# Code rows kept twice, and the mask products of a turn spread over eight 32x64 places: an attention and feed-forward kernel on one core

## The chip, the cores and the metric

The kernel runs on one core of a Trainium2 chip. The metric is the device time of one execution in microseconds (us). The engines are named as the profile names them: PE is TensorE (PEld its weight loads), DVE is VectorE, ACT is ScalarE, POOL is GpSimd, SP is SyncE, which here issues the transfers.

## What is computed

Attention in clusters, and then a feed-forward block. Every query and every key is assigned to the nearest of 16 centroids of its head; a query attends only to keys with the same assignment.

```python
batch, n_heads, seq, head_dim = (4, 8, 768, 64)      # q, k, v; n_clusters = 16
q_assign = np.argmax(np.einsum('bhsd,hcd->bhsc', q_n, c_n), axis=-1)
k_assign = np.argmax(np.einsum('bhsd,hcd->bhsc', k_n, c_n), axis=-1)
mask = q_assign[:, :, :, None] == k_assign[:, :, None, :]
scores = scale * np.matmul(q, k.transpose(0, 1, 3, 2))
scores = np.where(mask, scores, -1000000000.0)
attn = np.exp(scores - np.max(scores, axis=-1, keepdims=True))
attn = attn / (np.sum(attn, axis=-1, keepdims=True) + 1e-09)
out = np.matmul(attn, v)
# then, with x the heads side by side, (3072, 512)
h = x @ w_in                                         # (512, 2048)
return (h * (1.0 / (1.0 + np.exp(-1.702 * h)))) @ w_out
```

## The kernel before

The program has a fast path and a general one; the fast one runs, and the general one only if a check at the end says so. The fast path has two stages: attention (up to 353 us in the profile), and then the feed-forward block (L743 and L800), which the change doesn't touch.

**Tiling of the attention.** Heads are handled in pairs: 4 batches x 4 pairs = 16 pairs, the two heads of a pair (a = 0, 1) lying in partitions 0 to 63 and 64 to 127. For a pair, `T[p, 0]` and `T[p, 1]` hold queries and keys with the head dimension on the partitions. The queries of a pair are taken in two halves of 384, the keys in six blocks of 128; one half with one key block is a *unit*, 12 units a pair, 192 in all. Scores stand with keys on the partitions and queries along the row, for both heads: a PSUM tile `s` of 128 x 2 x 384, of which two exist, each head in a bank of its own.

**A turn** is two units. There are 96 turns, and the order of the work in them is written out by hand (L658 to L696):
- L453, `scores`: for each unit four fp32 products of 64 rows and 64 columns with 384 queries, one for each head and each half of the key block. An fp32 product leaves two records in the profile, so a turn has 16.
- L476, `part`: into the same PSUM tile the mask is added, again four products for each unit, in bf16, eight a turn (L467 in the first pair, see below).
- L484, `exps`: ScalarE takes the exponential of the unit, 128 x 768, to a tile `A`, of which there are four.
- L502, `add_up`: GpSimd adds up the exponentials over the key blocks (one of the twelve units goes to VectorE at L495).
- L518, `values`: exponentials of the turn before times the values, eight fp32 products of 64 rows and 64 columns, 16 records.
- Once in three turns L535 makes the row sums (128 rows, 64 columns) and VectorE normalises (L545 to L557), L527 copies the result out of PSUM; once in six L329 makes the products with the centroids for the next pair (128 rows, 32 columns), from which VectorE makes the assignments (L352 to L389). Between these, ScalarE and VectorE check and round the weights of the feed-forward block, step by step (L189 to L230).

**The mask.** Each key and query has a code, rank x 2^50 with ranks 1 to 16 for the clusters. For codes x (query) and y (key) the product is to be xy - x²/2 - y²/2 = -(x - y)²/2: nothing where they are equal, and hugely negative elsewhere. From the second pair on this is a product with three rows that count: on the key side y, y²'s multiple and the constant -0.5 x 2^50, on the query side x, the constant and x²'s multiple. They stand in tiles `rows_of[w, i]` (w = 0 for queries, 1 for keys; i changes with the pair), in the 64 partitions of their head, at 0, 1 and 32, and the other partitions are zero: the product at L476 takes all 64. The constants and zeros are written once at the start by GpSimd (L297, L299). The codes come for each pair through DRAM (`line`): four transfers at L398 write them, eight at L404 read them, one row of 768 each, issued by SyncE during the pair before.

The first pair's mask is made otherwise: L467 multiplies rows of 16 (one for each cluster) with 128 columns, four products a turn.

Names used for the prediction's steps: the *last turn's* `A` must be finished before L518; `s` of a unit must be read by L484 before the L453 two units later writes it again; `A` comes free when L518 and L502 have read it.

Of the kernel before, what the change touches and what calls it, by code (L numbers as in the profile page):

```python
# [18 lines left out]
def kernel(  # L19
    tc: tile.TileContext,  # L20
    q: bass.AP,
    k: bass.AP,
    v: bass.AP,
    centroids: bass.AP,
    moe_w_in: bass.AP,
    moe_w_out: bass.AP,
    out: bass.AP,
):

    args = (q, k, v, centroids, moe_w_in, moe_w_out, out)
    bad = fast(tc, *args)
    with tc.If(bad > 0):
        general(tc, *args)
# [3 lines left out]
def fast(  # L39
# [26 lines left out]
    nc = tc.nc  # L66

    B, H, S, D = q.shape
    NC = centroids.shape[1]
    DM, DF = moe_w_in.shape  # L70
    P = 128
# [10 lines left out]
    CODE = float(2 ** 50)  # L82
    NX = 6 * HP
    SQ = 32
# [137 lines left out]
    def check_w(i, raw, z):  # L222
# [39 lines left out]
    rows_of = {(w, i): hp1.tile([P, S], BF16, name=f"rows{w}{i}")  # L262
               for w in range(2) for i in range(2)}
# [22 lines left out]
    for a in range(2):  # L286
        rows = slice(a * D, (a + 1) * D)
        nc.vector.tensor_copy(
            out=cT[rows, :, a, :],
# [5 lines left out]

    for (w, _), rows in rows_of.items():
        nc.gpsimd.memset(rows, 0.0)  # L297
        for r in range(SQ * w, P, D):
            nc.gpsimd.memset(rows[r:r + 1, :], -0.5 * CODE)  # L299

    T, code, sT, hots = {}, {}, {}, {}

# [90 lines left out]
    def prep_spread(p):  # L393
        n = NJ * 4
        row = code.pop(p)
        line = dram.tile([2, n, P], BF16, name="line")
        for r in range(0, P, SQ):
            nc.sync.dma_start(  # L398
                out=line[:, :, r:r + SQ].rearrange("b n t -> n b t"),
                in_=row[r:r + n])  # L400
        for a in range(2):
            for w, b, to in ((0, 0, 1), (0, 1, SQ), (1, 0, 1), (1, 1, 0)):
                at, r = (w * 2 + a) * NJ, a * D + to
                nc.sync.dma_start(  # L404
                    out=rows_of[w, p % 2][r:r + 1, :],
                    in_=line[b, at:at + NJ, :].rearrange(
                        "j t -> (j t)")[None, :])

    def prep_hot(p):

# [18 lines left out]
    def hot_w(w, h, n):  # L429
# [3 lines left out]
    PREP = [lambda p, i=i: prep_turn(p, i) for i in range(4)]  # L433
    PREP += [prep_near, prep_assign,
             lambda p: (prep_hot if p == 0 else prep_spread)(p)]


# [5 lines left out]
    def split(g):  # L443
        return divmod(g, 2)
# [15 lines left out]
    def part(u):  # L460

        g, kt = divmod(u, NJ)
        p, h = split(g)
        if p == 0:
            for a in range(2):
                r = SQ * a
                nc.tensor.matmul(  # L467
                    out=s_of[u][:, a, :],
                    lhsT=hots[1][r:r + NC, kt * P:(kt + 1) * P],
                    rhs=hots[0][r:r + NC, h * HALF:(h + 1) * HALF],  # L470
                    start=False, stop=True)
            return
        for a in range(2):
            rows = slice(a * D, (a + 1) * D)
            for c in range(0, P, D):
                nc.tensor.matmul(  # L476
                    out=s_of[u][c:c + D, a, :],
                    lhsT=rows_of[1, p % 2][rows, kt * P + c:kt * P + c + D],
                    rhs=rows_of[0, p % 2][rows, h * HALF:(h + 1) * HALF],
                    start=False, stop=True)  # L480
# [156 lines left out]
    for p in range(1, NPAIR):  # L637
        for i in range(2 if p == 1 else 0, len(PREP)):
            t = 2 * TG * (p - 1) + (0, 0, 0, 0, 1, 2, 2)[i]
# [18 lines left out]
    for t in range(NT + 2):  # L658
# [5 lines left out]
        for u in us:  # L664
            part(u)
# [638 lines left out]
```

## Time and profile before

| | us |
|---|---|
| median of 3 runs | 939.36 (939.26 to 939.95) |
| profiled execution | 939.74 |
| its span | 937.8 |
| attention stage in it | to 353 |

A profile shows one execution. Busy time of an engine is the time in which any of its instructions runs. Matmuls are pipelined: their records overlap, and their ends are modelled, so the distance from the start of one group to the start of the next tells what a group costs. "64*64" is rows x columns of the stationary operand. A wait is put down to what ended it last.

Busy in one pair of the middle (205.2 to 225.7 us, 20.5 us): PE 20.36, DVE 18.43, ACT 14.46, POOL 18.50. Of the groups of instructions, these matter beside the ones that the prediction shows:

| line | what | count | mean ns |
|---|---|---|---|
| L453 | scores, 64*64, 64x384 fp32 | 1536 records | 494 |
| L518 | values, 64*64, 64x384 fp32 | 1536 records | 483 |
| L535 | row sums, 128*64, 128x384 fp32 | 128 records | 511 |
| L329 | centroids, 128*32, 128x192 fp32 | 240 records | 332 |
| L484 | exponential, 128x768 | 192 | 804 |
| L502 | additions, 128x384 fp32 | 252 + 32 | 1091, 1061 |
| L299 | memset of one row of 768 | 8 | 734 |
| L297 | memset of 128 rows of 768 | 4 | 742 |

### The profile page before, as it was taken

How to read it: one execution, taken by the hardware profiler on the slowest of the kernel's cores; microseconds unless marked ns; L12 is line 12 of the kernel's file. 1: busy time of each engine (PE TensorE's matmuls, PEld its weight loads, DVE VectorE, ACT ScalarE, POOL GpSimd, SP SyncE). 2: the span in 40 equal slices, each digit the busy share in tenths (PEclk: the TensorE clock that was granted, in tenths of full speed). 3: DMA queues.
4: the chain of work that ended last, by engine and by line, in shares of the span. 5: the costliest groups of instructions: out<-in, count | busy, mean ns of one | idle time of the engine just before them, and what ended most of it. 6: DMA issues, size and time to landing. Idle time of an engine off the chain costs nothing.

```text
span 937.8 us, 16591 instructions
## 1 busy us (share of the span) xinstructions
PE 920.5 (98%) x6469; PEld 578.4 (62%) x6469; DVE 624.0 (67%) x1077; ACT 326.0 (35%) x703; POOL 420.8 (45%) x440
## 2 busy tenths in 40 slices
PE   6999999999999999999999999999999999999997
PEld 2344444444444445558886557887557887556886
DVE  3999999989988896775345775344776343677331
ACT  3667767767776672221001221001222000232000
POOL 5899899899999996772001220001211000120000
PEclk9999999999999999999999999999999999999999
DMA  9465556566543210011000000000000000000000
GB/s 184 101 128 101 99 103 138 106 121 114 103 99 98 81 49 10 0 29 40 23 23 22 1 0 1 23 23 24 0 1 1 23 23 23 0 1 1 23 24 26
DMA packets 138215, 46.65 MB, mean 50 GB/s; under 512 B 127256, under 2 KB 132496, under 8 KB 138128
## 3 DMA queue, kind: packets, MB, share of 16 engines
q1 hardware_dynamic: 137984, 45.48, 22.1%
q8 instruction: 53, 0.87, 0.4%
q14 instruction: 34, 0.28, 0.1%
q10 hardware_dynamic: 144, 0.03, 0.0%
HBM read 37.44 MB, written 8.05 MB: 49 GB/s over the span
## 4 chain that ended last, share of the span: by engine, by line
PE 84%; POOL 4%; DVE 4%; issue 3%; ACT 2%; DMA 1%; SPq 1%; ACTq 0%; DVEq 0%; POOLq 0%
PE b L800 31%; PE b L743 31%; PE s L453 9%; PE o L518 7%; POOL sum L502 4%; PE m L535 2%; PE s L476 2%; ACT A L484 1%; PE m L329 1%; DMA line<-row 0%; DVE x L556 0%; SPq L404 0%; DMA raw<-in_moe_w_out_dram 0%; DVE e L200 0%; PE m L315 0%
## 5 line engine op out<-in xcount | busy, mean ns | idle before, releaser
L502 POOL TENSOR_TENSOR sum<-sum,A 128x384 f32<-128x384 f32 x252 | 266.2, 1091 | 33.6 <-ACT A L484 21.3
L589 POOL TENSOR_TENSOR W<-w_in 128x256 f32<-128x256 f32 x32 | 23.3, 729 | 379.6 <-PE b L743 379.4
L484 ACT ACTIVATE A<-s 128x768 f32<-128x768 f32 x192 | 145.1, 804 | 99.4 <-PE s L476 76.3
L734 DVE TENSOR_TENSOR G<-b,G 128x384 f32<-128x384 f32 x224 | 124.4, 556 | 62.7 <-PE b L743 50.4
L453 PE MATMUL s<-T,T 64*64 64x384 f32 x1536 | 145.8, 494 | 2.7 <-ACT A L484 0.7
L734 DVE TENSOR_TENSOR y<-b,y 128x256 f32<-128x256 f32 x72 | 29.5, 423 | 171.7 <-PE b L800 121.8
L518 PE MATMUL o<-A,inv 64*64 64x384 f32 x1536 | 141.5, 483 | 0.0
L579 ACT ACTIVATE th<-G 128x384 f32<-128x384 f32 x128 | 67.0, 523 | 208.8 <-DVE G L734 128.5
L580 DVE SCALAR_TENSOR_TENSOR G<-th,G 128x384 f32<-128x384 f32 x128 | 91.3, 713 | 23.0 <-ACT th L579 19.1
L453 PEld LDWEIGHTS s<-T,T 64*64 64x64 f32 x1536 | 52.7, 132 | 79.0 <-ACT A L484 51.3
L743 PE MATMUL b<-x,W 128*128 128x384 f32 x256 | 93.0, 486 | 0.0
L743 PE MATMUL b<-T,w_in 128*128 128x384 f32 x256 | 93.0, 486 | 0.0
L743 PE MATMUL b<-x,w_in 128*128 128x384 f32 x256 | 88.5, 486 | 0.0
L800 PE MATMUL b<-Z,G 128*128 128x256 f32 x384 | 86.8, 379 | 0.0
L800 PE MATMUL b<-w_out,G 128*128 128x256 f32 x384 | 84.8, 379 | 0.0
L518 PEld LDWEIGHTS o<-A,inv 64*64 64x64 f32 x1536 | 58.9, 133 | 38.3 <-issue 33.2
L800 PEld LDWEIGHTS b<-w_out,G 128*128 128x128 f32 x384 | 72.8, 190 | 10.9
L800 PEld LDWEIGHTS b<-Z,G 128*128 128x128 f32 x384 | 73.0, 190 | 9.9
L743 PEld LDWEIGHTS b<-x,W 128*128 128x128 f32 x256 | 48.6, 190 | 33.9
L743 PEld LDWEIGHTS b<-T,w_in 128*128 128x128 f32 x256 | 48.6, 190 | 33.9
L743 PEld LDWEIGHTS b<-x,w_in 128*128 128x128 f32 x256 | 48.6, 190 | 33.6 <-issue 0.6
L810 ACT COPY y<-b 128x256 f32<-128x256 f32 x12 | 4.5, 372 | 141.5 <-PE b L800 141.5
(120 smaller groups left out, 1130.6 us busy)
## 6 DMA issues: line engine op xcount, KB each, us to landing
raw<-in_moe_w_in_dram SPq DMA_DIRECT2D x16, 512.0 KB
raw<-in_moe_w_out_dram SPq DMA_DIRECT2D x16, 512.0 KB
inv<-in_v_dram SPq DMA_DIRECT2D x16, 384.0 KB
in<-in_q_dram SPq DMA_DIRECT2D x60, 96.0 KB
in<-in_k_dram SPq DMA_DIRECT2D x60, 96.0 KB
out_dram<-y SPq DMA_DIRECT2D x12, 256.0 KB
out_dram<-y SPq DMA_DIRECT2D x24, 128.0 KB
rows<-line SPq DMA_DIRECT2D x120, 1.5 KB
```

The source lines that it names most:

```text
L453: nc.tensor.matmul(out=ps[c:c + D, a, 0:HALF], lhsT=T[p, 1][rows, kt * P + c:kt * P + c + D], rhs=T[p, 0][rows, h * HALF:(h + 1) * HALF], ...
L476: nc.tensor.matmul(out=s_of[u][c:c + D, a, :], lhsT=rows_of[1, p % 2][rows, kt * P + c:kt * P + c + D], rhs=rows_of[0, p % 2][rows, h * HA ...
L484: nc.scalar.activation(out=A_of[u], in_=s_of.pop(u), func=AF.Exp, scale=SCALE)
L502: nc.gpsimd.tensor_tensor(out=sum_of[g][:, a], in0=(A_of[u - 1] if kt == 1 else sum_of[g])[:, a], in1=A_of[u][:, a], op=ALU.add)
L518: nc.tensor.matmul(out=o_of[g][a * D:(a + 1) * D, r, 0:HALF], lhsT=v_in[p][rows, a, kt, :], rhs=A[rows, a, :], start=(kt == 0), stop=(kt = ...
L535: nc.tensor.matmul(out=ps[a * D:(a + 1) * D, 0:HALF], lhsT=twos, rhs=sm[:, a, :], start=(i == 0), stop=(i == len(parts) - 1))
L579: nc.scalar.activation(out=t, in_=h, func=AF.Tanh, scale=1.702)
L580: nc.vector.scalar_tensor_tensor(out=g, in0=t, scalar=1.0, in1=h, op0=ALU.add, op1=ALU.mult)
L589: engine.tensor_tensor(out=o, in0=a, in1=b, op=(ALU.add if op == "+" else ALU.subtract))
L734: nc.vector.tensor_tensor(out=o, in0=p, in1=a, op=ALU.add)
L743: nc.tensor.matmul(out=ps[:, 0:HALF], lhsT=a[:, c], rhs=x(c), start=(c == 0), stop=(c == 1))
L800: nc.tensor.matmul(out=ps[:, 0:DN], lhsT=a(f // 4)[:, f % 4], rhs=z(f), start=(f == 0), stop=(f == FB - 1))
```

## The change

The three rows of a head that count stand at 0, 1 and 2 in place of 0, 1 and 32, and they are kept twice: in partitions 0 to 2 and again in 32 to 34 of the head's 64. The product takes only these three rows, those of the first copy for the even unit of a turn and those of the second for the odd one. So the eight products of a turn have eight different places: four groups of rows (head and unit) by two groups of columns (half of the key block). Each transfer at L404 writes two partitions, 32 apart, from the same row of DRAM; the constants are written at four places of each of the four tiles in place of two, as one row (queries) or three (keys, of which two are overwritten by the codes). The first pair is as before.

```diff
     for (w, _), rows in rows_of.items():
         nc.gpsimd.memset(rows, 0.0)
-        for r in range(SQ * w, P, D):
-            nc.gpsimd.memset(rows[r:r + 1, :], -0.5 * CODE)
+        for r in range(0, P, SQ):
+            nc.gpsimd.memset(rows[r:r + 1 + 2 * w, :], -0.5 * CODE)
...
         for a in range(2):
-            for w, b, to in ((0, 0, 1), (0, 1, SQ), (1, 0, 1), (1, 1, 0)):
+            for w, b, to in ((0, 0, 1), (0, 1, 2), (1, 0, 1), (1, 1, 0)):
                 at, r = (w * 2 + a) * NJ, a * D + to
                 nc.sync.dma_start(
-                    out=rows_of[w, p % 2][r:r + 1, :],
+                    out=rows_of[w, p % 2][r:r + SQ + 1:SQ, :],
                     in_=line[b, at:at + NJ, :].rearrange(
-                        "j t -> (j t)")[None, :])
+                        "j t -> (j t)")[None, :].broadcast_to((2, S)))
...
         for a in range(2):
-            rows = slice(a * D, (a + 1) * D)
+            r = a * D + u % 2 * SQ
+            rows = slice(r, r + 3)
             for c in range(0, P, D):
                 nc.tensor.matmul(
                     out=s_of[u][c:c + D, a, :],
```

## The prediction, made before the changed kernel was run

> **What bounds the kernel now.** I read the page first, for the shares and for the chain that ended last.
>
> ```profile
> PE 920.5 (98%) x6469; PEld 578.4 (62%) x6469; DVE 624.0 (67%) x1077; ACT 326.0 (35%) x703; POOL 420.8 (45%) x440
> ...
> PE b L800 31%; PE b L743 31%; PE s L453 9%; PE o L518 7%; POOL sum L502 4%; PE m L535 2%; PE s L476 2%; ACT A L484 1%; PE m L329 1%; DMA line<-row 0%; DVE x L556 0%; SPq L404 0%; DMA raw<-in_moe_w_out_dram 0%; DVE e L200 0%; PE m L315 0%
> ```
>
> TensorE bounds it over the whole span, but the change lies in the attention stage alone, which ends at 353 us; from there L743 and L800 run as they do now. The mask products, L476, hold 2% of the chain. The groups by form give their durations, and beside them those of the first pair's mask products at L467, the only products in the trace with at most 32 rows:
>
> ```profile
> L476 PE MATMUL s<-rows,rows 64*64 64x384 bf16 x720 | 45.9, 323 | 0.9 <-DMA rows<-line 0.9
> ...
> L467 PE MATMUL s<-hots,hots 16*128 16x384 bf16 x24 | 3.2, 351 | 0.9 <-ACT hots L426 0.9
> ```
>
> 720 products in eights are 90 turns. What a turn costs is read in the timeline of TensorE, from start to start (first number start, second length to the modelled end of the last record):
>
> ```profile
> 203.52 1.47 PE L518 MATMUL o<-A,inv 64*64 64x384 f32 x16
> 205.13 1.57 PE L453 MATMUL s<-T,T 64*64 64x384 f32 x16
> 206.52 0.51 PE L476 MATMUL s<-rows,rows 64*64 64x384 bf16 x8
> ...
> 212.79 1.47 PE L453 MATMUL s<-T,T 64*64 64x384 f32 x16
> 214.08 0.51 PE L476 MATMUL s<-rows,rows 64*64 64x384 bf16 x8
> 214.40 1.47 PE L518 MATMUL o<-A,inv 64*64 64x384 f32 x16
> 215.69 1.47 PE L453 MATMUL s<-T,T 64*64 64x384 f32 x16
> ...
> 217.31 1.47 PE L518 MATMUL o<-A,inv 64*64 64x384 f32 x16
> 218.71 0.87 PE L535 MATMUL m<-sum,twos 128*64 128x384 f32 x4
> 219.50 1.52 PE L453 MATMUL s<-T,T 64*64 64x384 f32 x16
> ```
>
> A plain turn is 1.29 (L453) + 0.32 (L476) + 1.29 (L518) = 2.90 us. The eight mask products go in two rounds of four, 0.16 each; each lasts 0.32 and overlaps the next group, because all three lines use 64*64 operands. Where the operand's shape changes this overlap goes: L518 to L535 takes 217.31 to 218.71 = 1.40 instead of 1.29, though only the rows change (64 to 128, still 64 columns). L535 has two records in turn on each of its two places, 4 x 0.16 = 0.64, and takes 0.79 to the next line. So a change costs 0.11 to 0.15. The first pair's turns show a product of few rows between the same two neighbours:
>
> ```profile
> 26.36 1.47 PE L453 MATMUL s<-T,T 64*64 64x384 f32 x16
> 27.76 0.50 PE L467 MATMUL s<-hots,hots 16*128 16x384 bf16 x4
> 28.19 1.52 PE L518 MATMUL o<-A,inv 64*64 64x384 f32 x16
> 29.53 1.47 PE L453 MATMUL s<-T,T 64*64 64x384 f32 x16
> ```
>
> Here L453 takes 1.40, the mask 0.43 (two rounds of two, again 0.32 of streaming) and L518 1.34, because its first weights are no longer loaded ahead: 3.17 us, 0.27 more than a plain turn.
>
> **The change, part by part.** *Products in 32x64.* They take 3 rows where L453 and L518 keep 64, so I expect the change of shape twice in each of the 90 turns. The trace has no 32x64 product; the bounds come from the rows above.
> - L453 to L476: 1.40 instead of 1.29, +0.11.
> - L476 to L518: all eight in one round. Lower end: L467's 0.43 less one round, 0.43 - 0.16 = 0.27. Upper end: the eight of now have a length of 0.51, of which 0.32 + 0.16 are one product and one round, so starting four costs some 0.027, about 0.009 a step. Eight then end after 0.32 + 7 x 0.009 = 0.385, and L518 starts 0.07 before the modelled end of such a group (27.76 + 0.50 against 28.19): 0.31. I take the middle, 0.29, instead of 0.32: -0.03.
> - L518 to L453: 1.34 instead of 1.29, +0.05.
>
> Sum: 3.03 us a turn, **+0.13** (+0.11 to +0.15). Half of the streaming is saved and more than that is given back at the two seams.
>
> [...]
>
> *What hides part of it.* A pair of heads is six turns, and at the last two ScalarE decides:
>
> ```profile
> 200.73 1.51 ACT L484 ACTIVATE A<-s 128x768 f32<-128x768 f32 x2 [1.57 <-PE s L476]
> ...
> 204.28 1.49 ACT L484 ACTIVATE A<-s 128x768 f32<-128x768 f32 x2
> ```
>
> From 200.73 ScalarE works without a pause (exponentials, check, the two passes over a weight block) until the first exponential at 204.28 is done; L453 at 205.13 waits for that: 203.52 to 205.13 is 1.61, 0.32 above 1.29. This ScalarE stretch keeps its length and starts only 0.11 later (the even unit's four products still go first). So those two turns cost +0.11 together, instead of 0.26; without this cover they would cost 0.26. A pair costs 4 x 0.13 + 0.11 = 0.63. From 61.5 to 266.8 us there are ten such pairs of 20.5: **+6.3**.
>
> *Later pairs.* From 260 on, GpSimd's additions and its weight sums run without a gap until 319:
>
> ```profile
> 272.50 8.50 POOL L502 TENSOR_TENSOR sum<-sum,A 128x384 f32<-128x384 f32 x8
> 280.96 1.97 POOL L502 TENSOR_TENSOR sum<-A 128x384 f32<-128x384 f32 x2
> 282.88 9.25 POOL L502 TENSOR_TENSOR sum<-sum,A 128x384 f32<-128x384 f32 x8
> ```
>
> TensorE waits for them at L535 (280.37, 291.15, 302.64 and 313.74), 3.8 us in all above the 0.79 of an undisturbed L535. What the 13 turns here lose, 13 x 0.13 = 1.7 at most, comes off these waits: 0; without the cover 1.7. After 316 there are ten turns, of which two stretches (the turns at 326.0 and 329.0; those from 336.1 to 342.0) end at a wait for ScalarE and cost 0.11 as a whole: 3 x 0.13 + 0.11 + 0.13 + 0.11 + 0.13 = **+0.9**.
>
> *First pairs.* Until 59.7 VectorE sets the pace without a pause and then the transfers of the second pair's codes; TensorE waits 0.85 for them at its L476. Six turns at 0.13 are 0.8 and vanish in that wait: 0, at most +0.8.
>
> *Transfers.* Each of the eight L404 issues of a pair now writes two partitions. Issuing takes 0.25 us; the nearest row with more partitions is L398 with 0.36. Between 0 and 8 x 0.11 = 0.9, and it counts only where the codes are late, at 59.7: I take **+0.2**. In the other pairs they are issued some 5 us ahead of need. Behind them on SyncE's queue stand the weight loads of L170 (at 220.80 after the issues of 218.40); only the last of them, at 327.4, is on the chain, which is in the 0.9.
>
> *Memsets.* L299 fills 16 slices instead of 8, of at most 3 partitions, 0.73 us each like now: GpSimd is busy until 19.7 instead of 13.4. Its next work begins at 21.72 after 8.32 us of idleness: 0. If they took twice as long each (0.73 is the figure for one row and 0.74 for 128, so this is excluded by the rows), the first addition would be late.
>
> **Sum:** 6.3 + 0.9 + 0.2 = +7.4 us, 946.8 from the median of 939.36. The profiled execution took 939.74, of which 937.8 is the span, 0.4 above that median; its span should grow to 945.2. Own range: with 0.11 a turn 10 x 0.55 + 0.8 = +6.3; with 0.15 a turn, the dearer transfers and GpSimd's cover gone 10 x 0.71 + 1.0 + 0.9 + 1.7 = +10.7. So 945.7 to 950.1.
>
> **Rivals.**
> 1. *No seam* (faster). 64 rows to 32 at equal columns keeps the overlap. For it: no row shows this very change. Against: L518 to L535 also changes rows alone and pays 0.11. Then L476 takes 0.16 to 0.20 instead of 0.32, -0.12 to -0.16 in four turns of a pair; the ScalarE turns give nothing, and GpSimd's stretch nothing: ten pairs give -4.8 to -6.4, with the end some -5.5 in the middle: 933.8. It decides from the point where both seams cost under 0.12 together.
> 2. *Four places at once* (slower still). The seams are paid and the eight products go in two rounds. For it: no more than four matmuls run together anywhere in this trace. Against: L467 shows rows 0 and 32 side by side (four products in 0.50; one after another they would need 0.80). A turn is 3.17, +0.27. Two ScalarE turns have 0.54 against a cover of 0.32: 0.22. A pair is 4 x 0.27 + 0.22 = 1.30, ten pairs 13.0; the end 1.8, the first pairs 1.6 - 0.85 = 0.8, transfers 0.2: +15.8, so 955.2.
> 3. *One seam only.* Entering 32x64 is free and leaving it is not: 1.29 + 0.29 + 1.34 = 2.92, +0.02 a turn, ten pairs +0.8, with the transfers 940.4: no difference.
> 4. *The tiles aren't taken*, the products stay 64*64: no seam, no gain, 939.5. The operands begin at multiples of 32 partitions and have 3 rows, which speaks against it; I count it with the third.
>
> **Chances.** Forecast 0.70, no seam 0.10, four places 0.14, one seam or none of the change 0.06. A difference of 0.2% (1.9 us) is about what a measurement of this kernel can tell from none. Faster 0.10; within it 0.05 (the third and fourth, nearly whole); slower 0.85. The range of eight in ten takes the forecast's own range, some room below it for a cheaper seam, and reaches up over the second rival: 943.5 to 955.5.
>
> **What would show it.** L476 as 3*64, one round of eight with some 0.38 instead of 0.51; 1.40 from L453 to L476, 0.27 to 0.31 from L476 to L518, 1.34 from L518 to L453; a pair of 21.2 instead of 20.5 in the middle; the stretch from 266.8 to 314.7 as long as before; the 0.32 by which L453 waits for ScalarE once a pair cut to about 0.17. The forecast is wrong if L453 to L476 stays at 1.29, or if L476's eight need 0.43 to L518. If the turns are as written but the total isn't, ScalarE's or GpSimd's cover was misjudged.

## The result, and the profile after

The changed kernel takes 948.32 us (median of 4 runs, 946.69 to 951.22) against 939.31 us before: a ratio of 1.0095, 95% interval 1.0083 to 1.0108. It is slower. The runs lie 4.5 us apart, where those before lay 0.7 apart; that spread has a cause of its own, which the experiments separate from the rest. The execution in the profile is the longest of the four, 951.22 us with a span of 949.3.

The change adds a line, so L476 is now L477, L518 is L519, L535 is L536 and L743 is L744. In the page, the chain that ended last has moved more onto TensorE, 93% in place of 84%. GpSimd, which held 4%, holds 0%, and issuing the codes at L404 holds 1% where it held 0%:

```profile
PE 93%; DVE 4%; DMA 1%; SPq 1%; issue 0%; ACT 0%; POOL 0%; DVEq 0%
PE b L801 31%; PE b L744 30%; PE o L519 13%; PE s L453 12%; PE m L536 3%; PE s L477 3%; PE m L329 1%; SPq L404 1%; DMA line<-row 1%; DMA rows<-line 0%; DVE x L557 0%; DVE e L200 0%; PE m L315 0%; DMA short<-in_centroids_dram 0%; DVE best L361 0%
```

The feed-forward stage is untouched: 364.39 to 949.3 us is 584.9, before it was 352.95 to 937.8, 584.9. All 11.4 us of this execution are lost in the attention. Turns in the middle, from the timeline of TensorE (start, length, line; distances from start to start count):

```profile
222.41 1.47 PE L453 MATMUL s<-T,T 64*64 64x384 f32 x16
223.81 0.37 PE L477 MATMUL s<-rows,rows 3*64 3x384 bf16 x8
224.11 1.52 PE L519 MATMUL o<-A,inv 64*64 64x384 f32 x16
225.46 1.47 PE L453 MATMUL s<-T,T 64*64 64x384 f32 x16
...
234.19 1.52 PE L519 MATMUL o<-A,inv 64*64 64x384 f32 x16
235.71 1.58 PE L453 MATMUL s<-T,T 64*64 64x384 f32 x16
```

The eight products do run in one round: their group has a length of 0.37 where it had 0.51. But a turn is 1.40 + 0.30 + 1.34 = 3.04 us, where it was 2.90. The mask group took 0.32 to the next line and takes 0.30, so 0.02 is gained. The rest is lost at the two changes of shape in a turn, which are called seams below: 0.11 where L453 is followed by another shape, and 0.05 where L519 starts without weights loaded ahead. (The first of them are loaded at 74.70, at which its products start; before, at 73.24 for products from 73.40.) Once a pair L453 still waits for ScalarE: 234.19 to 235.71 is 1.52, 0.18 above 1.34. A pair takes 21.22 us (214.49 to 235.71), before it was 20.55.

Ten pairs at 0.67 are 6.7 us. Most of the rest is at the start. There TensorE waits for the codes of the third pair (p = 2; the prediction and the expectations call them the second pair's, which is off by one):

```profile
59.86 0.35 PE L477 MATMUL s<-rows,rows 3*64 3x384 bf16 x2 [0.29 <-issue]
62.04 0.54 PE L477 MATMUL s<-rows,rows 3*64 3x384 bf16 x6 [1.83 <-DMA rows<-line]
62.50 2.84 PE L519 MATMUL o<-A,inv 64*64 64x384 f32 x16
65.12 1.53 PE L453 MATMUL s<-T,T 64*64 64x384 f32 x16
```

Before, those products went on at 59.70; now at 62.04. And then L519 takes 2.62 us in place of 1.34. The table of windows, whose columns are busy time by engine (PE, PEld, DVE, ACT, POOL), TensorE's granted clock, the DMA share and GB/s, says why:

```profile
60.00:62.00 2.00, 0.21 (x2) 0.00 (x0) 1.93 (x4) 0.56 (x2) 2.00 (x3) 0.96 0.27 29
62.00:63.00 1.00, 0.96 (x10) 0.44 (x14) 1.00 (x2) 0.33 (x1) 1.00 (x2) 0.50 0.64 172
63.00:64.00 1.00, 1.00 (x12) 0.41 (x8) 0.32 (x1) 1.00 (x2) 0.62 (x1) 0.50 0.91 295
64.00:65.00 1.00, 1.00 (x12) 0.33 (x8) 0.79 (x1) 0.18 (x1) 0.00 (x0) 0.50 0.98 381
65.00:66.00 1.00, 1.00 (x16) 0.50 (x12) 0.17 (x1) 0.59 (x2) 0.00 (x0) 0.88 1.15 276
```

TensorE idles nearly the whole of 60 to 62 and gets half the clock for the three microseconds after it: another 1.3 us. The reason why the codes come late stands in SyncE's queue, here the changed kernel:

```profile
51.52 1.54 SPq L398 DMA_DIRECT2D line<-row  x4
56.23 4.54 SPq L404 DMA_DIRECT2D rows<-line  x8
```

and here the kernel before:

```profile
51.40 1.54 SPq L398 DMA_DIRECT2D line<-row  x4
55.73 2.66 SPq L404 DMA_DIRECT2D rows<-line  x8
```

The four writes are issued at the same time and the reads begin 0.5 later; but the eight reads take 4.54 us to issue instead of 2.66. A single issue is 0.452 us (median) instead of 0.252. In the same execution the codes of the fifth pair are late too, by 0.76 at 106.81.

### The profile page after: what moved, and what is told of

Read it like the earlier page. It is cut to its first block, busy times and chain, and to the rows that moved or that the text cites. A ratio compares the mean times of both kernels' runs of the same rounds, so it can differ in the third digit from the quotient of the medians.

```text
span 949.3 us, 16599 instructions
## 1 busy us (share of the span) xinstructions
PE 932.1 (98%) x6469; PEld 557.7 (59%) x6469; DVE 630.1 (66%) x1077; ACT 325.9 (34%) x703; POOL 426.3 (45%) x448
## 4 chain that ended last, share of the span: by engine, by line
PE 93%; DVE 4%; DMA 1%; SPq 1%; issue 0%; ACT 0%; POOL 0%; DVEq 0%
PE b L801 31%; PE b L744 30%; PE o L519 13%; PE s L453 12%; PE m L536 3%; PE s L477 3%; PE m L329 1%; SPq L404 1%; DMA line<-row 1%; DMA rows<-line 0%; DVE x L557 0%; DVE e L200 0%; PE m L315 0%; DMA short<-in_centroids_dram 0%; DVE best L361 0%
## 5 line engine op out<-in xcount | busy, mean ns | idle before, releaser
L590 POOL TENSOR_TENSOR W<-w_in 128x256 f32<-128x256 f32 x32 | 24.0, 751 | 379.7 <-PE b L744 379.6
L519 PE MATMUL o<-A,inv 64*64 64x384 f32 x1536 | 147.1, 499 | 0.0
L453 PE MATMUL s<-T,T 64*64 64x384 f32 x1536 | 145.6, 494 | 0.8 <-ACT A L485 0.7
L453 PEld LDWEIGHTS s<-T,T 64*64 64x64 f32 x1536 | 53.0, 133 | 77.1 <-ACT A L485 45.7
L744 PE MATMUL b<-x,W 128*128 128x384 f32 x256 | 93.0, 486 | 0.0
L744 PE MATMUL b<-T,w_in 128*128 128x384 f32 x256 | 93.0, 486 | 0.0
L744 PE MATMUL b<-x,w_in 128*128 128x384 f32 x256 | 88.6, 486 | 0.0
L519 PEld LDWEIGHTS o<-A,inv 64*64 64x64 f32 x1536 | 49.7, 133 | 50.9 <-issue 50.1
L744 PEld LDWEIGHTS b<-x,W 128*128 128x128 f32 x256 | 48.6, 190 | 33.9
L744 PEld LDWEIGHTS b<-T,w_in 128*128 128x128 f32 x256 | 48.6, 190 | 33.9
L744 PEld LDWEIGHTS b<-x,w_in 128*128 128x128 f32 x256 | 48.6, 190 | 33.6 <-issue 0.6
```

What stands on the lines that cost most here:

```text
L453: nc.tensor.matmul(out=ps[c:c + D, a, 0:HALF], lhsT=T[p, 1][rows, kt * P + c:kt * P + c + D], rhs=T[p, 0][rows, h * HALF:(h + 1) * HALF], ...
L519: nc.tensor.matmul(out=o_of[g][a * D:(a + 1) * D, r, 0:HALF], lhsT=v_in[p][rows, a, kt, :], rhs=A[rows, a, :], start=(kt == 0), stop=(kt = ...
L590: engine.tensor_tensor(out=o, in0=a, in1=b, op=(ALU.add if op == "+" else ALU.subtract))
L744: nc.tensor.matmul(out=ps[:, 0:HALF], lhsT=a[:, c], rhs=x(c), start=(c == 0), stop=(c == 1))
```

## The experiments

**The copies without the small tiles.** Both copies are kept and moved, and the product takes all 64 rows again. Both copies are then multiplied, so the mask is twice as large; it is zero in the same places.

```diff
             r = a * D + u % 2 * SQ
-            rows = slice(r, r + 3)
+            rows = slice(a * D, (a + 1) * D)
```

> The data of the changed kernel (both copies, doubled transfers and memsets) with the products of 64 rows of before; both copies are multiplied, so the mask is twice as large, zero where codes agree. Theory (two seams in every turn carry most of the loss, the transfers the rest): a plain turn is 2.90 us again; L404 issues take 0.45 us, so the codes of the second pair come some 2.3 us later than before and TensorE waits for them; perhaps one stretch at a lower clock behind that wait. 941 to 943.5 us. Rival A (the transfers carry the whole loss): 947 or more. Rival B (the array alone, transfers free): 939.3.

Measured: 943.15 us (941.59 to 944.46) against 939.37, ratio 1.0039 (1.0027 to 1.0051). From its timeline of TensorE:

```profile
62.22 0.51 PE L477 MATMUL s<-rows,rows 64*64 64x384 bf16 x6 [2.18 <-DMA rows<-line]
62.41 1.61 PE L519 MATMUL o<-A,inv 64*64 64x384 f32 x16
...
71.39 1.47 PE L453 MATMUL s<-T,T 64*64 64x384 f32 x16
72.69 0.51 PE L477 MATMUL s<-rows,rows 64*64 64x384 bf16 x8
73.01 1.47 PE L519 MATMUL o<-A,inv 64*64 64x384 f32 x16
74.30 1.47 PE L453 MATMUL s<-T,T 64*64 64x384 f32 x16
```

The turn is back at 2.91 us, so nothing of the 0.14 belongs to the copies; and the wait for late codes is all there, 2.18 us, without any small tile. Both rivals fall: the transfers don't carry the whole loss, and they are not free. Two shorter waits for codes follow later, 1.34 us at 104.58 and 1.00 at 291.17. After the first wait L519 takes its usual 1.29, and the clock stays whole (its column is the one before the last two):

```profile
60.00:62.00 2.00, 0.04 (x2) 0.00 (x0) 1.90 (x4) 0.52 (x2) 2.00 (x2) 1.00 0.02 6
62.00:63.00 1.00, 0.78 (x14) 0.69 (x18) 1.00 (x2) 0.33 (x1) 1.00 (x2) 1.00 0.83 176
```

**The small tiles without the copies.** Rows 0 to 2 are kept once and both units take them: 32x64 with four places.

```diff
-        for r in range(0, P, SQ):
+        for r in range(0, P, D):
             nc.gpsimd.memset(rows[r:r + 1 + 2 * w, :], -0.5 * CODE)
...
-                    out=rows_of[w, p % 2][r:r + SQ + 1:SQ, :],
+                    out=rows_of[w, p % 2][r:r + 1, :],
                     in_=line[b, at:at + NJ, :].rearrange(
-                        "j t -> (j t)")[None, :].broadcast_to((2, S)))
+                        "j t -> (j t)")[None, :])
...
-            r = a * D + u % 2 * SQ
+            r = a * D
             rows = slice(r, r + 3)
```

> Rows 0 to 2 kept once, one partition for each transfer as before, both units multiply the same three rows: tiles of 32x64, but only four places, so two rounds of four. Theory: the seams stay and a round is added: L477's eight have a length of about 0.51 in place of 0.37, 0.43 to 0.46 to L519, a turn of 3.17 to 3.20, a pair of some 21.8 to 22.0 us in the middle, L404 issues of 0.25 us and no late codes; 951 to 955 us. Rival (the eight places bring nothing, the rest of the loss is transfers): a turn of 3.04 and 946 us.

Measured: 954.09 us (953.65 to 954.91), ratio 1.0156 (1.0142 to 1.0169).

```profile
70.60 1.47 PE L453 MATMUL s<-T,T 64*64 64x384 f32 x16
72.00 0.52 PE L477 MATMUL s<-rows,rows 3*64 3x384 bf16 x8
72.45 1.52 PE L519 MATMUL o<-A,inv 64*64 64x384 f32 x16
73.79 1.47 PE L453 MATMUL s<-T,T 64*64 64x384 f32 x16
```

Two rounds between two seams: 0.45 to L519 and 3.19 a turn. A pair takes 21.83 us. So the eight places are worth 0.15 a turn, about what one of the two rounds of before takes (half of 0.32), and the seams take 0.29 away. No codes are late in this kernel, and its runs lie 1.3 us apart.

**Why an issue is dear.** First guess: because one row of DRAM is read for two partitions. In this kernel each transfer takes a code and its square, two different rows, to the two partitions where they are wanted; for queries these are neighbours, for keys they are two apart. The constants are written as three rows for both (not shown).

```diff
-            for w, b, to in ((0, 0, 1), (0, 1, 2), (1, 0, 1), (1, 1, 0)):
-                at, r = (w * 2 + a) * NJ, a * D + to
+            for w in range(2):
+                for e in range(2):
+                    at, r = (w * 2 + a) * NJ, a * D + e * SQ
...
-                    out=rows_of[w, p % 2][r:r + SQ + 1:SQ, :],
...
+                        out=rows_of[w, p % 2][r:r + 2 + w:1 + w, :],
+                        in_=line[:, at:at + NJ, :].rearrange(
+                            "b j t -> b (j t)"))
```

> Products as in the changed kernel; each transfer at L404 still writes two partitions, but a code row and its square from two rows of DRAM, with no row read twice: again eight issues for a pair. Theory (the turn is the array's, and late codes cost 2.3 us and more): if the issue is dear because one row is read for two partitions, it falls to 0.25 to 0.36 us, the codes of the second pair come about as before, and the time is 945.5 to 946.5 us with runs closer together. If every partition costs 0.2 us in an issue, it stays 0.45 us and the time 947 to 949 us. Turns of 3.04 in both cases.

Measured: 949.16 us (947.99 to 950.90), ratio 1.0103 (1.0088 to 1.0119): no better, and slightly above the 947 to 949 us expected for issues that stay dear. The view of the tile `rows` gives the issues (shortest, median, longest in ns):

```profile
L405 SPq DMA_DIRECT2D rows<-line x120: 223/482/675, 29.2 to 337.6; - x120
```

Not reading a row twice is not the answer. But the shortest issue, 0.223 us, is as short as one for a single partition (0.215 to 0.263 in the kernel before), so two partitions need not be dear. The third pair's issues, of which the chain that ended last holds the first seven, from 55.30 on, show what separates them. In order they take 0.23, 0.26, 0.58, 0.54, 0.42, 0.32 and 0.56 us: the first two and the fifth and sixth are for queries, whose partitions are neighbours, the others for keys, whose partitions are two apart. So within one kernel the issues to partitions apart are the dear ones. The 0.42 of the fifth, to neighbours, isn't explained. This run also has a stretch at half the clock (0.50 from 62 to 64 us) behind a wait of only 1.0 us.

**The changed kernel once more**, on the same chip as the three above.

> The changed kernel once more, beside the others on one chip. Theory: turns of 3.04 and pairs of 21.2 us in the middle, the end of the attention as long as before (86.2 us from the last such pair on), and a spread of some us between runs that comes from late codes at the start of single pairs (second and fourth in the first profile) and a lower clock behind such a wait; 946.5 to 951 us. Rival (the spread lies elsewhere): the pairs in the middle differ from run to run.

Measured: 949.65 us (947.19 to 952.16), ratio 1.0118 (1.0101 to 1.0134). The profiled execution is the shortest, 947.19 with a span of 945.2, and in it the line in DRAM was written sooner, so the reads could be issued from 53.92 on, not from 56.23 (why the line is written sooner in one execution than in another isn't known):

```profile
58.14 1.47 PE L453 MATMUL s<-T,T 64*64 64x384 f32 x16
59.54 0.50 PE L477 MATMUL s<-rows,rows 3*64 3x384 bf16 x8
59.97 1.52 PE L519 MATMUL o<-A,inv 64*64 64x384 f32 x16
61.36 1.57 PE L453 MATMUL s<-T,T 64*64 64x384 f32 x16
```

At the place where the first execution lost 3.6 us there is hardly a wait: the mask group takes 0.43 to L519, 0.13 more than a plain turn's. Its pairs in the middle take 21.22 us as in the first: the spread lies where the theory puts it, and not in the turns.

**Neighbouring partitions.** The code is written to the line twice, before and behind its square, and the rows are put in the order square, code, constant for queries and constant, code, square for keys. Then each transfer goes to two neighbours, and there are still eight. (The loop that this replaces is the changed kernel's; the wider row and the constants, written as three rows, are not shown.)

```diff
...
+        nc.vector.tensor_copy(
+            out=row[:, 0:3:2],
+            in_=turned[:, None, :].broadcast_to((P, 2, SQ)))
...
-        line = dram.tile([2, n, P], BF16, name="line")
+        line = dram.tile([3, n, P], BF16, name="line")
...
+            for w in range(2):
+                for e in range(2):
+                    at, r = (w * 2 + a) * NJ, a * D + e * SQ + w
+                    nc.sync.dma_start(
+                        out=rows_of[w, p % 2][r:r + 2, :],
+                        in_=line[1 - w:3 - w, at:at + NJ, :].rearrange(
+                            "b j t -> b (j t)"))
```

> Products as in the changed kernel, both copies; the rows are put in another order, the code is kept twice in the line in DRAM (the cast writes it to two places, L398 writes half as much again), so that each of the eight transfers writes two partitions that are next to each other. Theory (an issue is dear where the two partitions lie apart): issues of 0.25 to 0.4 us, the codes of the second pair at most 1 us late, runs closer together, 946 to 948 us, turns of 3.04. Rival (each partition costs): 0.45 us and 947 to 952 us.

Measured: 946.91 us (946.08 to 946.99) against 939.67, ratio 1.0074 (1.0060 to 1.0088).

```profile
L407 SPq DMA_DIRECT2D rows<-line x120: 223/253/332, 30.1 to 333.9; - x120
```

An issue costs 0.253 us, as much as for one partition. Of the waits for codes some 0.2 us are left (the third pair's mask group, at 59.75, takes 0.52 to the next line), and the runs lie 0.9 us apart instead of 4.5. What is left, 7.2 us, is the turns: ten pairs at 0.67, and 0.5 before them (L329 of the third pair stands at 65.63, before at 65.14), in which the 0.2 lies.

**The same for the kernel before.** Its products of 64 rows and one copy, with code and square in one transfer, four a pair. The line is written as in the kernel above (not shown).

```diff
-            for w, b, to in ((0, 0, 1), (0, 1, SQ), (1, 0, 1), (1, 1, 0)):
-                at, r = (w * 2 + a) * NJ, a * D + to
+            for w in range(2):
+                at, r = (w * 2 + a) * NJ, a * D + w
...
-                    out=rows_of[w, p % 2][r:r + 1, :],
+                    out=rows_of[w, p % 2][r:r + 2, :],
...
+                    in_=line[1 - w:3 - w, at:at + NJ, :].rearrange(
+                        "b j t -> b (j t)"))
```

> Products of 64 rows and one copy as before the change, but code and square of a head go in one transfer to two partitions next to each other: four issues for a pair in place of eight. Theory: plain turns of 2.90; issuing a pair's codes takes some 1.2 us in place of 2.3, so the wait of 0.85 for the second pair's codes goes: 938.4 to 939.3 us. Rival (issues are not what makes the codes late, the writing of the line is): 939.3 as before.

Measured: 939.29 us (938.44 to 939.85) against 939.67, ratio 0.9998 (0.9989 to 1.0007): no difference that can be measured.

```profile
58.48 0.51 PE L478 MATMUL s<-rows,rows 64*64 64x384 bf16 x8
58.80 1.47 PE L520 MATMUL o<-A,inv 64*64 64x384 f32 x16
```

In its profile the wait of 0.85 before 59.70 is gone and the span is 937.1 instead of 937.8. But the spans of the kernel before lie between 936.7 and 938.2, so one trace proves nothing, and the times don't confirm a gain. No version here is measurably faster than the kernel before.

## Why the prediction was right

It said 946.8 us, own range 945.7 to 950.1; measured 948.32. By its steps:

- *The seams.* 1.40, 0.27 to 0.31 and 1.34 were forecast; 1.40, 0.30 and 1.34 came, +0.14 a turn where 0.13 was taken. Shown by three kernels side by side: 64 rows in two rounds 2.90, 3 rows in two rounds 3.19, 3 rows in one round 3.04. For 64x64 to 32x64, for which the trace of before had no row, the changed kernel's now has one: 1.40 instead of 1.29. The trace shows the lost overlap; it doesn't show what the array does in it.
- *The round of eight.* Its group is 0.37 long and a single product of it 0.345, so a further place costs (0.37 - 0.345) / 7 = 0.004 us. I had taken 0.009, an estimate from the rounds of four. A product behind a seam is longer, though (0.345 against 0.322), and the two errors nearly cancel.
- *ScalarE's cover.* Two turns of a pair were to cost +0.11 together, with a wait of about 0.17 left; 0.18 is left. A pair costs +0.67 against 0.63, ten pairs 6.7 against 6.3.
- *GpSimd's cover and the end.* 0 and +0.9 were forecast. From the last undisturbed pair's end to L744 it took 86.16 us before (266.79 to 352.95) and 86.22 after (278.17 to 364.39), and 86.20 in the second execution: less than 0.1 in all. The end did cost its 0.9: from the end of the stretch behind GpSimd to the last turn's L453 it took 30.40 us before (315.55 to 345.95) and 31.30 after (326.51 to 357.81). But GpSimd gave as much back, in two places that the forecast counted as nothing. The stretch itself is 0.4 shorter (266.79 to 315.55 is 48.76, 278.17 to 326.51 is 48.34). The waits at L536 show how:

```profile
292.28 0.87 PE L536 MATMUL m<-sum,twos 128*64 128x384 f32 x4
293.08 1.52 PE L453 MATMUL s<-T,T 64*64 64x384 f32 x16
...
302.65 1.35 PE L536 MATMUL m<-sum,twos 128*64 128x384 f32 x4
303.93 0.86 PE L329 MATMUL m<-T,cT 128*32 128x192 f32 x16
```

These two take 0.80 and 1.28, the next two 1.39 and 1.56, in all 1.9 us above four times 0.79; before it was 3.8. Slower turns ahead of the stretch left GpSimd less far behind when it began: its weight sums at L589 (now L590) start 2.02 us after 266.79 before (at 268.81), and 1.71 us after 278.17 now (at 279.88). The other place is the last row sums ahead of the feed-forward stage, which waited for an addition of GpSimd's: 1.25 us before (351.70 to 352.95), 0.75 now (363.64 to 364.39).
- *The first pairs.* The turns' loss before 59.7 was to vanish in the wait for codes. In the second execution, where codes come in time, the pair's L329 stands at 65.41 against 65.14: 0.3 is left of 0.8.
- *The transfers*: this term was mis-sized, and its place too narrow. I took 0.2, bounded by issues of 0.36 from L398. An issue is 0.452 where the two partitions lie 32 apart and 0.253 where they are neighbours; L398's partitions are neighbours and no measure of the first. Eight issues take 1.6 to 1.9 us more, and they delay not only the third pair's codes but in some executions also the fifth's. Its reads were not issued some 5 us ahead of need, as the working says, but 4.0 (96.44 to 100.40 before). With the turns nearly alone at a ratio of 1.0074 and the changed kernel at 1.0095 and 1.0118, the median pays some 2 to 3 us for late codes (948.32 - 1.0074 x 939.31 = 2.1, and 949.65 - 1.0074 x 939.37 = 3.3 for the second set); a single execution between hardly anything (946.69) and nearly 6 (952.16), if nothing else separates the runs; only two of the eight were profiled. So the total is partly luck: 2 to 3 us stood against a term of 0.2, and the 0.9 that GpSimd gave back made up for a part of it. The measured time lies in the upper half of the range, which was drawn so far up for other costs (0.15 a turn, GpSimd's cover gone) that didn't come.
- *The memsets.* GpSimd is done at 19.75 and next needed at 21.89: nothing, as forecast.
- *The rivals.* No seam, one seam and an unchanged shape are excluded by the turns. Four places at once is excluded for the change itself, and the kernel that was built that way took 954.1 where the working gave 955.2.

## What to carry to other kernels

By what this case shows, packing small products into more places of the array, between groups of another shape, pays only if it saves more streaming than the two changes of shape cost; here one saved round of 0.15 us stands against seams of 0.29 a turn, and the price of a seam could be read beforehand from other neighbours of different shapes in the trace (1.40 from L518 to L535 and from L453 to L467, 1.34 for L518 behind L467, against 1.29). Price a changed transfer by its issue too, and by a row that is like it in the spacing of its partitions. Where a median moves and the runs spread at once, there may be two losses: look for the one that differs between two profiles of the same kernel.

## What was not expected of the hardware

- Issuing a transfer to two partitions took 0.253 us where they were neighbours and 0.452 where they were 32 apart; for one partition it was 0.252. In the kernel with pairs of rows, in the pair whose issues are given above, it took 0.54 to 0.58 where they were two apart and 0.23 to 0.32 where they were neighbours, but for one of 0.42, and why isn't known. So partitions that aren't neighbours made an issue dear, but not in proportion to their distance.
- After a wait of 1.8 us (changed kernel) and one of 1.0 us (the kernel with pairs of rows) TensorE's granted clock was 0.50 for some three microseconds (from 62 to 65 us in the first; from 62 to 64 in the second, with 0.79 over the two microseconds before and 0.72 in the one behind); after waits of 2.2 and 1.3 us (64 rows with copies) it stayed at 1.00, and after one of 1.0 us in that kernel L519 took its usual 1.29. So the length of the wait alone doesn't decide. The products differ too, 3 rows in the first two kernels and 64 in the third, and that wasn't tried apart. What does decide isn't shown by any run here.
